# A linear-attention kernel with a folded feed-forward: one weight turned by VectorE in blocks, sign bits on GpSimd, seven products for one more chunk index, and a new order

## The chip, the cores and the metric

The kernel runs on one core of one Trainium2 chip. The metric is the device time of one execution in microseconds (us); below 2% a change of the median is called "within 2%".

## What is computed

Attention first: B=4 batches, H=8 heads, S=768 steps, D=48 numbers per head, with a state that decays by a constant w per head and row. Then a feed-forward on the 3072 rows of 384 numbers that come out of it.

```
for t in range(S):
    cur = einsum('bhd,bhe->bhde', u * kt, vt)
    y[:, :, t] = einsum('bhd,bhde->bhe', rt, state + cur)
    state = w * state + einsum('bhd,bhe->bhde', kt, vt)
x = y.transpose(0, 2, 1, 3).reshape(3072, 384)
a = x @ w1          # 384 x 1024
b = x @ w2          # 384 x 1024
out = ((a * b) @ w3) @ w_out     # 1024 x 1024, 1024 x 384
```

The four weights arrive as 64-bit floats; r, k, v, w, u as 32-bit floats.

## The kernel before, in words

**Units and chunks.** The steps are cut into six chunks of 128 steps; a chunk of one batch is a unit, so there are 24 units, four to a chunk index c. A unit's attention: k and r are scaled by tables of powers of w (`scale`, k in the order, L422 on VectorE), turned (by TensorE for units 0 to 4, T and R; by VectorE in 32x32 blocks with a trip through DRAM for the rest, x, y, z, l), multiplied (A, U, S, V), masked (m), and its rows are turned and put into `xT` (yt, yx). `odd_values` (vs, L678) copies v's odd heads to the other half of the partitions, on ScalarE.

**Opening.** Up to L306 a first section builds the tables: VectorE doubles powers in `both` (L292, L294), copies their first half to the second (L297, on ScalarE L298), TensorE turns four blocks for each of k and r (L303), and ScalarE puts both results into `pn_in` (L304).

**Weights.** There are 32 pieces: 8 strips of w1 and w2 (768 KB each), 8 row blocks of w_out (384 KB), 16 half row blocks of w3 (512 KB). A piece is fetched (W, L234) into one of three buffers and made a 32-bit float in five steps: magnitude (M, ScalarE L370), sign bits (N, VectorE L375), high part (H, VectorE L378), low part (L, ScalarE L382, the last to read the buffer), total (Q, VectorE L385). Since no function stands between w3 and w_out, the kernel folds them into one 1024 x 384 weight w34: for each of 8 row blocks j of w3, TensorE turns it (G, L398, eight 128x128 transposes in two halves), ScalarE takes the turned blocks out of PSUM (K, L403), TensorE multiplies by w_out (F, L408), ScalarE keeps the result (X, L411).

**Products.** For chunk indices 0 and 1, a and b are plain products (a, b, L740, up to 512 columns wide), with one ScalarE copy and one VectorE multiplication for each block of 128 rows. For chunk indices 2 to 5 they are made with seven products in place of eight over two thirds of the depth, from sums of weights (wa, wb) and of x (xs): `product_half` (pa, pb, L885 and L889, 256 columns wide) and `gather_half` (ga, gb, L900 to L916). The product with w34 uses seven products for all chunks (s, B, P, E, D). Z puts idle products on TensorE (L921).

**Order.** `ORDER` (L23) is a list of some 1,400 words; each names a step and its indices. The engines work in order, so the list fixes the order of the work of TensorE, ScalarE, VectorE and of SP, which issues the DMAs. When the opening has found w in a normal range, the listed program runs; else a plain one.

Of the kernel before, what the change touches and what calls it, by code (L numbers as in the profile page):

```python
# [8 lines left out]
F32 = mybir.dt.float32  # L9
BF16 = mybir.dt.bfloat16  # L10
I32 = mybir.dt.int32
U32 = mybir.dt.uint32
# [6 lines left out]
PE, ACT, DVE, SP = (getattr(mybir.EngineType, x) for x in ("PE", "Activation", "DVE", "SP"))  # L19
# [4 lines left out]
k.0 uw Z.1.0 R.0 vs.0 T.0 k.1 kr.2 U.0 t.0 v.2 r.0 i.0 T.1 j.0 ku.0 A.0 R.1 N.0 v.1 Au.0 t.1 r.1 S.0 m.0 kr.3 ku.1  # L24
mo.0 k.2 Z.4.0 A.1 M.0 Au.1 fe.0 R.2 W.1 m.1 vs.2 T.2 mo.1 U.2 W.2 t.2 H.0 V.0 r.2 Y.0 v.3 A.2 i.2 j.2 ku.2 U.1 yt.0
kr.4 i.1 j.1 S.2 L.0 Au.2 k.3 yx.0 vs.1 Z.1.0 R.3 m.2 T.3 M.1 mo.2 S.1 fe.2 fe.1 t.3 V.2 N.1 V.1 r.3 H.1 Y.2 A.3 W.3
Q.0 ku.3 yt.2 N.2 kr.5 vs.3 Z.2.0 Au.3 Y.1 m.3 yx.2 Z.2.0 U.3 mo.3 M.2 yt.1 v.5 i.3 k.4 S.3 yx.1 L.1 a.0.0.0 fe.3 H.2
Q.1 M.3 V.3 W.4 T.4 N.3 Y.3 R.4 H.3 kr.6 t.4 yt.3 b.0.1.0 r.4 j.3 ku.4 k.5 A.4 v.6 cz.1 L.3 Au.4 x.5 b.0.0.0 yx.3 L.2
Q.3 a.0.1.1 M.4 N.4 W.5 Q.2 vs.5 W.6 H.4 c.0.0.0 c.0.1.1 Z.3.0 b.0.2.2 m.4 v.4 L.4 mo.4 W.7 vs.6 Q.4 d.5 a.0.2.2
u.0.0.0 y.5 N.5 M.5 H.5 U.5 c.0.2.2 a.0.1.0 u.0.2.2 L.5 ub N.6 M.6 Q.5 b.0.1.1 vs.4 W.8 H.6 b.0.4.2 c.0.1.0 u.0.1.0  # L30
L.6 u.0.1.1 Q.6 W.9 M.7 N.7 a.0.4.2 H.7 z.5 e.5 L.7 f.5 Q.7 M.8 a.0.7.2 c.0.4.2 N.8 H.8 M.9 N.9 W.10 L.8 H.9 W.11 Q.8
L.9 b.0.6.2 Q.9 c.0.7.2 W.12 h.5 kr.7 l.5 d.6 e.6 f.6 a.0.0.1 M.10 N.10 H.10 b.0.7.2 N.11 M.11 kr.8 u.0.4.2 L.10 H.11
c.0.0.1 L.11 Q.10 N.12 M.12 Q.11 a.0.5.2 W.13 H.12 L.12 W.14 k.7 Q.12 W.15 b.0.0.1 d.7 c.0.5.2 e.7 kr.10 f.7 A.5
u.0.0.1 b.0.3.2 i.5 M.13 N.13 H.13 N.14 L.13 m.5 M.14 W.16 H.14 a.0.6.2 M.15 Q.13 L.14 N.15 W.17 H.15 Q.14 L.15 Q.15
W.18 c.0.6.2 j.5 b.0.5.2 u.0.6.2 M.16 N.16 H.16 u.0.7.2 M.17 a.0.3.2 N.17 L.16 H.17 W.19 Q.16 L.17 N.18 M.18 W.20 Q.17
G.0.0 c.0.3.2 H.18 G.0.1 K.0.0 U.4 u.0.3.2 L.18 k.6 K.0.1 W.21 F.0 N.19 M.19 kr.9 Q.18 H.19 N.20 M.20 i.4 L.19 H.20
W.22 Q.19 L.20 Q.20 M.21 W.23 N.21 G.1.0 X.0 H.21 G.1.1 K.1.0 U.6 j.4 K.1.1 G.2.0 x.6 L.21 F.1 K.2.0 W.24 Q.21 M.22
y.6 N.22 H.22 k.8 L.22 M.23 W.25 N.23 H.23 Q.22 L.23 N.24 W.26 G.2.1 Q.23 M.24 S.4 z.6 x.7 K.2.1 G.3.0 X.1 G.3.1 fe.4
H.24 K.3.0 F.2 M.25 N.25 u.0.5.2 L.24 H.25 K.3.1 Q.24 L.25 y.7 Q.25 M.26 W.28 N.26 H.26 W.27 d.8 l.6 e.8 kr.11 G.4.1
G.4.0 L.26 x.8 A.6 K.4.0 V.4 i.6 X.2 F.3 Y.4 cz.0 v.7 M.28 m.6 K.4.1 j.6 z.7 M.27 N.28 H.28 Q.26 L.28 Q.28 N.27 H.27  # L40
S.5 X.3 G.6.0 vs.7 fe.5 y.8 G.5.0 K.6.0 W.29 P.0.0.0 L.27 Q.27 W.30 V.5 W.31 l.7 yt.4 Y.5 G.5.1 g.6 yt.5 v.8 F.4 z.8
N.29 M.29 f.8 yx.4 H.29 yx.5 N.30 L.29 d.9 K.5.0 Q.29 K.5.1 N.31 g.7 S.6 e.9 G.6.1 fe.6 V.6 K.6.1 U.7 Y.6 v.9 M.30 A.7
k.9 F.6 M.31 X.4 m.7 kr.12 l.8 i.7 j.7 vs.8 x.9 vs.9 H.30 y.9 H.31 L.30 Q.30 L.31 U.8 X.6 Q.31 S.7 A.8 fe.7 k.10 V.7
yt.6 z.9 m.8 G.7.0 yx.6 i.8 G.7.1 K.7.0 F.5 j.8 K.7.1 g.8 x.10 v.10 s.0.1.0 y.10 s.0.1.1 Y.7 s.0.1.2 l.9 f.9 d.10 yt.7
X.5 e.10 kr.13 ps f.10 yx.7 g.9 s.0.1.3 z.10 d.11 b.1.0.2 e.11 vs.10 f.11 d.12 e.12 a.1.0.2 b.1.1.2 c.1.0.2 u.1.0.2
a.1.5.2 a.1.1.2 c.1.5.2 b.1.2.2 c.1.1.2 u.1.1.2 a.1.2.2 a.1.4.2 c.1.2.2 u.1.2.2 S.8 c.1.4.2 U.9 fe.8 l.10 A.9 k.11
b.1.4.2 i.9 kr.14 j.9 m.9 x.11 U.10 A.10 u.1.4.2 y.11 V.8 k.12 F.7 v.11 i.10 kr.15 j.10 m.10 Y.8 z.11 x.12 vs.11
a.1.3.2 B.0 X.7 E.0.0.0 s.0.0.0 y.12 B.1 a.1.6.2 s.0.0.1 c.1.3.2 B.3 B.2 s.0.0.2 P.0.0.2 c.1.6.2 wb.0 wb.1 P.0.1.4
s.0.0.3 wa.0 P.0.0.3 wa.1 wb.3 P.0.1.2 wa.3 E.0.0.2 U.11 E.0.0.3 P.0.0.4 k.13 x.13 P.0.1.0 E.0.0.4 y.13 b.1.6.2
E.0.1.0 E.0.1.2 b.1.5.2 u.1.6.2 P.0.1.1 u.1.5.2 s.1.0.0 P.0.0.5 s.1.0.1 s.1.0.3 a.1.7.2 s.1.0.2 E.0.1.1 E.0.0.6  # L50
E.0.0.5 D.0.0.0 P.0.0.1 wa.2 c.1.7.2 P.0.0.6 E.0.0.1 b.1.3.2 E.0.0.7 D.0.0.1 P.0.1.6 u.1.3.2 P.0.1.3 P.1.0.0 E.0.1.3
E.0.1.4 yt.8 E.1.0.0 P.0.1.5 g.10 b.1.7.2 E.0.1.6 E.0.1.7 f.12 yx.8 D.0.1.1 d.13 e.13 kr.16 P.1.1.0 u.1.7.2 s.1.1.0
P.1.0.4 s.1.1.1 E.1.1.0 s.1.1.3 P.1.0.2 s.1.1.2 wb.2 P.1.0.6 E.1.0.2 E.0.1.5 D.0.1.0 P.1.0.3 P.1.0.5 E.1.0.3 E.1.0.4
P.1.1.1 E.1.0.6 E.1.0.5 D.1.0.0 P.1.1.4 E.1.1.1 P.1.0.1 P.1.1.2 E.1.0.1 E.1.0.7 D.1.0.1 S.9 E.1.1.2 P.1.1.3 fe.9 l.11
z.12 V.9 E.1.1.3 Y.9 A.11 P.1.1.5 i.11 j.11 yt.9 m.11 v.12 P.1.1.6 yx.9 E.1.1.6 g.11 E.1.1.4 E.1.1.5 S.11 D.1.1.0
E.1.1.7 S.10 D.1.1.1 fe.11 V.11 fe.10 l.12 f.13 V.10 v.14 Y.11 U.12 v.13 vs.12 Y.10 yt.11 k.14 z.13 pa.2.0.0 yx.11
x.14 A.12 ga.2.0.0 yt.10 i.12 pa.2.0.1 yx.10 m.12 g.12 j.12 xs.2.0 S.12 y.14 xs.2.1 U.13 fe.12 xs.2.2 ga.2.0.5 V.12
xs.2.3 g.13 pa.2.0.5 d.14 v.15 e.14 kr.17 pa.2.1.4 Y.12 f.14 pa.2.0.4 ga.2.0.1 d.15 l.13 e.15 pa.2.0.6 ga.2.0.3 vs.13
A.13 z.14 f.15 yt.12 ga.2.0.2 i.13 pb.2.0.0 vs.15 m.13 yx.12 pa.2.0.7 j.13 g.14 k.15 pa.2.0.3 ga.2.0.4 kr.18 x.15
# [46 lines left out]
def kernel(  # L106
# [60 lines left out]

# [885 lines left out]
```

## Time and profile before

| what | value |
|---|---|
| runs | 507.63, 500.76, 507.02 us; median 507.02 |
| profiled execution | 501.81 us, its span 500.1 us |
| TensorE busy | 483.8 us |
| VectorE, ScalarE, GpSimd busy | 319.5, 202.7, 4.4 us |
| granted TensorE clock | 0.999 |

The profile is one execution, and its span runs from the first to the last instruction; 1.7 us of the execution's time lie around it. The three runs lie 6.9 us apart, and the profiled execution lies near the lowest. An fp32 product is two passes of TensorE, so 42 products of 512 columns show as 84 instructions; a transpose is one pass. Instructions of one engine overlap by a little, so that a group's busy time can be below count times mean.

### The profile page before, as it was taken

What the parts mean: (1) busy time and instruction counts of PE and PEld (TensorE: products, weight loads), DVE (VectorE), ACT (ScalarE), POOL (GpSimd) and SP (SyncE); (2) the same over time, 40 slices, a digit from 0 to 9 for tenths busy, and PEclk for the clock granted to TensorE, in tenths of its full rate; (3) what the DMA queues carried; (4) which work ended last, traced back from release to release, by engine and by line L of the source; (5) the groups of instructions that cost most, each with busy time, mean ns of one, the idle gap of its engine ahead of it and who ended that gap; (6) DMA issues with size and microseconds to landing.
All of it is one profiled execution on the core that took longest, in us unless ns stands there. A gap on an engine that the chain in (4) does not pass through costs nothing.

```text
span 500.1 us, 11978 instructions
## 1 busy us (share of the span) xinstructions
PE 483.8 (97%) x5066; PEld 384.4 (77%) x5066; DVE 319.5 (64%) x648; ACT 202.7 (41%) x470; POOL 4.4 (1%) x17
## 2 busy tenths in 40 slices
PE   6899999989999999999999999999999999999995
PEld 5786545657644586898888889989998889888895
DVE  5799999985951874539967894539462564524352
ACT  3887646768632100206852633062422232322300
POOL 3000000000000000000000000000000000000000
PEclk9999999999999999999999999999999999999999
DMA  8969787896620600216734435002300020000002
GB/s 193 241 167 287 209 224 227 250 262 172 159 64 1 174 33 20 59 49 177 167 108 108 113 99 139 32 33 70 90 33 31 1 81 17 27 25 0 2 1 69
DMA packets 97279, 52.72 MB, mean 105 GB/s; under 512 B 78144, under 2 KB 88640, under 8 KB 97216
## 3 DMA queue, kind: packets, MB, share of 16 engines
q1 hardware_dynamic: 96592, 51.85, 37.6%
q8 instruction: 42, 0.69, 0.6%
q14 instruction: 21, 0.17, 0.1%
q10 hardware_dynamic: 624, 0.00, 0.1%
HBM read 39.65 MB, written 12.19 MB: 104 GB/s over the span
## 4 chain that ended last, share of the span: by engine, by line
PE 86%; DMA 5%; DVE 4%; ACT 2%; issue 1%; SPq 0%; ACTq 0%; DVEq 0%
PE ps_accB L885 8%; PE ps_b L740 7%; PE ps_a L740 7%; PE ps_w L408 5%; PE ps_a11b L798 3%; PE ps_s1t L798 3%; PE ps_s4b L798 3%; PE ps_s3t L798 3%; PE ps_a22t L798 3%; PE ps_s2t L798 3%; PE ps_a12b L798 3%; PE ps_Ab L885 3%; PE ps_accB L889 3%; PE ps_a L551 3%; PE ps_accC L885 3%; PE ps_Aa L885 3%
## 5 line engine op out<-in xcount | busy, mean ns | idle before, releaser
L740 PE MATMUL ps_b<-xT,w 128*128 128x512 f32 (+1 forms) x108 | 44.4, 550 | 0.9 <-ACT a L746 0.7
L740 PE MATMUL ps_a<-xT,w 128*128 128x512 f32 (+1 forms) x108 | 43.7, 547 | 0.0
L408 PE MATMUL ps_w<-wo,w3T 128*128 128x384 f32 x128 | 43.0, 489 | 0.0
L885 PE MATMUL ps_accB<-x,w 128*128 128x256 f32 x128 | 36.5, 387 | 0.0
L740 PEld LDWEIGHTS ps_a<-xT,w 128*128 128x128 f32 x108 | 20.3, 190 | 20.5 <-issue 18.4
L408 PEld LDWEIGHTS ps_w<-wo,w3T 128*128 128x128 f32 x128 | 23.7, 190 | 15.1
L452 ACT ACTIVATE ynat<-vnat,dg 128x48 f32<-128x48 f32 x144 | 34.4, 325 | 0.8 <-PE ps_x L710 0.7
L740 PEld LDWEIGHTS ps_b<-xT,w 128*128 128x128 f32 x108 | 19.9, 190 | 18.7 <-issue 15.8
L508 ACT COPY kT<-tt 128x1024 f32<-128x1024 f32 x19 | 19.9, 1047 | 23.3 <-PE ps_y L671 21.0
L382 ACT ACTIVATE t<-raw 128x512 uint32<-128x512 uint32 (+2 forms) x32 | 22.6, 710 | 14.6 <-DVE wo L378 6.7
L885 PEld LDWEIGHTS ps_accB<-x,w 128*128 128x128 f32 x128 | 23.2, 190 | 5.0 <-ACT u2a L902 1.1
L422 DVE TENSOR_TENSOR krs<-krin,pn_in 128x768 f32<-128x768 f32 x24 | 22.9, 953 | 5.9 <-PE ps_a L544 3.3
L749 DVE TENSOR_TENSOR abt<-ps_b,a 128x512 f32<-128x512 f32 (+1 forms) x18 | 11.2, 628 | 20.5 <-ACT a L746 14.0
L746 ACT COPY a<-ps_a 128x512 f32<-128x512 f32 (+1 forms) x18 | 9.5, 535 | 33.4 <-PE ps_a L740 33.3
L716 ACT COPY xT<-ps_x 128x384 f32<-128x384 f32 x24 | 11.4, 478 | 28.8 <-PE ps_x L710 28.6
L678 ACT COPY vodd<-vnat 64x192 f32<-64x192 f32 x48 | 16.8, 350 | 13.8 <-DMA vnat<-in_v_dram 12.8
L551 PE MATMUL ps_a<-kT 64*64 64x64 f32 x768 | 16.8, 222 | 3.0 <-ACT kT L508 1.7
L813 ACT COPY m<-ps_a11b 128x192 f32<-128x192 f32 x12 | 3.8, 320 | 38.7 <-PE ps_a11b L798 38.7
L492 DVE STREAM_TRANSPOSE tr<-krs 128x768 f32<-128x768 f32 x19 | 18.4, 970 | 1.1 <-DMA scratch<-tr 0.9
L602 DVE COPY_PREDICATED AT<-later,ps_a 128x512 f32<-128x512 int32 x24 | 17.5, 730 | 2.5 <-PE ps_a L572 1.4
L889 PE MATMUL ps_accB<-xT,w 128*128 128x256 f32 x64 | 19.0, 379 | 0.0
L889 PE MATMUL ps_accC<-xT,w 128*128 128x256 f32 x64 | 19.0, 379 | 0.0
(191 smaller groups left out, 1069.0 us busy)
## 6 DMA issues: line engine op xcount, KB each, us to landing
raw<-in_moe_w_dram SPq DMA_DIRECT2D x16, 512.0 KB, 4.9
scratch<-tr SPq DMA_DIRECT2D x19, 384.0 KB, 3.1
raw<-in_moe_w_dram SPq DMA_DIRECT2D x8, 768.0 KB, 5.8
tt<-scratch SPq DMA_DIRECT2D x38, 128.0 KB, 3.1
krin<-in_k_dram SPq DMA_DIRECT2D x24, 192.0 KB, 3.8
krin<-in_r_dram SPq DMA_DIRECT2D x24, 192.0 KB, 4.3
vnat<-in_v_dram SPq DMA_DIRECT2D x24, 192.0 KB, 3.8
raw<-in_moe_w_out_dram SPq DMA_DIRECT2D x8, 384.0 KB, 3.6
```

Of the source, the lines that this page charges most:

```text
L382: nc.scalar.activation(out=part["t", i], in_=words(i)[0], func=COPY, scale=2.0 ** -29)
L408: nc.tensor.matmul(ps, lhsT=w3T[j][:, kc, :], rhs=wo[kc], start=(kc == 0), stop=(kc == KF - 1))
L422: nc.vector.tensor_mul(krs[n % NS][:, which, :, :D], kr[:, which], pn[:, which, :, :D])
L452: nc.scalar.activation(out=ynat[n][:, h, :], in_=vnat[n % NV][:, h, :], func=COPY, scale=dg[n][:, h:h + 1])
L492: nc.vector.transpose(out=blocks[n].rearrange("x m e t -> x e m t"), in_=krs[n % NS][:, :, :, :D])
L508: nc.scalar.copy(out=turned(n).rearrange("x g p (z t) -> x (g p) z t", t=Q), in_=tts.rearrange("x z e t -> x e z t"))
L551: nc.tensor.matmul(upper(n)[rows(a ^ i), i, p, :], lhsT=kT[n][rows(i), p, rows(a)], rhs=rT[n][rows(i), p, rows(a)], start=True, stop=True)
L602: nc.vector.copy_predicated(AT[n], later.bitcast(I32)[:, None, None, :].to_broadcast([C, 2, NP, T]), upper(n))
L740: nc.tensor.matmul(ps, lhsT=(w1 if x == "a" else w2)[:, z, q, js], rhs=xT[c][:, q, ts], start=(q == 0), stop=(q == KM - 1))
L798: nc.tensor.matmul(ps, lhsT=operand(c, j // 2, a)[:, j % 2, m * C:(m + 1) * C], rhs=w34[:, KH * (x == 1) + j, :DH] if x < 2 else made[b][: ...
L885: nc.tensor.matmul(ps, lhsT=quarter(w, g, i, x), rhs=(b11, b21, b22, t4, b12, t2, t3)[x], start=x in (0, 4) and i == 0, stop=True, skip_gr ...
L889: nc.tensor.matmul(ps, lhsT=wide_of[w][:, g + half * HZ, 2, i * P:(i + 1) * P], rhs=xT[c][:, 2, side * TH:(side + 1) * TH], start=False, s ...
```

## The change

- The 64 transposes of w3 on TensorE and the 16 ScalarE copies (K) go. `fold_turn` is now one VectorE transpose of 32x32 blocks for each half, SBUF to SBUF, 16 in all. So that blocks end in the right place, each fetch of a w3 piece becomes two DMAs of 256 KB that lay the four column blocks of 32 rows on the partitions, and w_out's rows are spread in the same way.
- Sign bits: N (VectorE, 32 times) goes; p is new: GpSimd multiplies the piece's high words, read as floats, by 0.0.
- vp is new: v's odd heads of units 0 to 5 are copied by GpSimd, not by ScalarE.
- Chunk index 1 uses pa, pb, ga, gb, xs: the eight pairs a.1, b.1 with c.1 and u.1 go. The sums of weights and of x, and two of the m1 tiles, now lie in the pool of the four w3 tiles, which stays open.
- Opening: the copies at L297 and L298 go, the eight transposes become 16 products of 64 columns each with the identity, and the second result is put by VectorE.
- Unit 0's scaling is split in two (ka, kb). Z: six words (13 idle products) become two (2 products).
- The list is new, and GpSimd is now also bound to it.

```diff
-k.0 uw Z.1.0 R.0 vs.0 T.0 k.1 kr.2 U.0 t.0 v.2 r.0 i.0 T.1 j.0 ku.0 A.0 R.1 N.0 v.1 Au.0 t.1 r.1 S.0 m.0 kr.3 ku.1
...
-k.9 F.6 M.31 X.4 m.7 kr.12 l.8 i.7 j.7 vs.8 x.9 vs.9 H.30 y.9 H.31 L.30 Q.30 L.31 U.8 X.6 Q.31 S.7 A.8 fe.7 k.10 V.7
-yt.6 z.9 m.8 G.7.0 yx.6 i.8 G.7.1 K.7.0 F.5 j.8 K.7.1 g.8 x.10 v.10 s.0.1.0 y.10 s.0.1.1 Y.7 s.0.1.2 l.9 f.9 d.10 yt.7
-X.5 e.10 kr.13 ps f.10 yx.7 g.9 s.0.1.3 z.10 d.11 b.1.0.2 e.11 vs.10 f.11 d.12 e.12 a.1.0.2 b.1.1.2 c.1.0.2 u.1.0.2
...
+v.1 kr.2 uw ka.0 k.1 vp.0 U.0 T.0 i.0 kb.0 T.1 t.0 v.2 j.0 p.0 ku.0 Z.1.1 R.0 kr.3 U.1 r.0 vp.1 i.1 t.1 j.1 Z.1.1 A.0
...
+p.14 d.8 e.8 H.14 L.14 p.16 M.16 Q.14 W.17 A.5 M.15 p.15 H.16 b.0.6.2 c.0.6.2 i.5 L.16 m.5 W.19 j.5 H.15 a.0.3.2 L.15
...
+p.30 V.6 m.7 M.31 F.6 i.7 j.7 v.9 H.30 Y.6 L.30 H.31 l.8 Q.30 G.7.0 L.31 s.0.1.0 vs.9 U.8 wa.0 A.8 X.6 wa.1 F.5 Q.31
+G.7.1 wa.3 wb.0 wa.2 s.0.1.1 i.8 k.9 yt.6 X.5 F.7 wb.1 yx.6 g.8 wb.3 x.9 k.10 y.9 s.0.1.2 j.8 m.8 S.7 s.0.0.0 X.7 U.9
+z.9 fe.7 B.0 V.7 P.0.1.0 Y.7 B.1 yt.7 v.10 E.0.1.0 s.0.0.1 pa.1.0.0 yx.7 xs.1.0 E.0.0.0 P.0.1.2 ga.1.0.0 xs.1.1 xs.1.2
...
-            queue.dma_start(out=landed[i], in_=pieces[i])
+            if i < NAB + KF:
+                queue.dma_start(out=landed[i] if i < NAB else landed[i][:, 0], in_=pieces[i])
+            else:
+                j, z = divmod(i - NAB - KF, NW3)
+                for f in range(2):
+                    queue.dma_start(out=landed[i][:, 0, f * DF // NBLOCK:(f + 1) * DF // NBLOCK],
+                                    in_=moe_w3[j * P:(j + 1) * P].rearrange("(f r) (q x) -> f q r x", r=Q, q=NBLOCK)[2 * z + f])
...
-        nc.vector.tensor_copy(out=both[:, 0, :, T:], in_=both[:, 0, :, :T])
-        nc.scalar.copy(out=both[:, 1, :, T:], in_=both[:, 1, :, :T])
...
-                nc.tensor.transpose(ps[:, p, :], both[:, g, p, :], ident)
-            nc.scalar.copy(out=pn_in[:, g].rearrange("t h d -> t (h d)"), in_=ps.rearrange("x p t -> x (p t)"))
+                for a in range(2):
+                    nc.tensor.matmul(ps[rows(a), p, :], lhsT=both[:, g, p, :T], rhs=ident, start=True, stop=True)
+            put = nc.vector.tensor_copy if g else nc.scalar.copy
+            put(out=pn_in[:, g].rearrange("t h d -> t (h d)"), in_=ps.rearrange("x p t -> x (p t)"))
...
+        def sign_by_scale(i, pool=False):
+            m, n = landed[i].shape[1:]
+            part["t", i] = once.tile([P, RAW], U32, tag="cv", bufs=2, name="t")[:, :m * n].rearrange("p (m n) -> p m n", m=m)
+            if pool:
+                nc.gpsimd.tensor_scalar(part["t", i].bitcast(F32), words(i)[1].bitcast(F32), 0.0, None, ALU.mult)
+            else:
+                nc.scalar.activation(out=part["t", i].bitcast(F32), in_=words(i)[1].bitcast(F32), func=COPY, scale=0.0)
...
         def fold_turn(j, h):
-            pst["w3", j, h] = ps = psT.tile([P, KF // 2, P], F32, tag="t", name=f"ps_w3T{j}_{h}")
-            for q in range(KF // 2):
-                kc = h * (KF // 2) + q
-                nc.tensor.transpose(ps[:, q, :], w3n[j][:, kc * P:(kc + 1) * P], ident)
-
-        def fold_put(j, h):
-            if h == 0:
-                w3T[j] = once.tile([P, KF, P], F32, tag="w3", bufs=4 if fast else 3, name=f"w3T{j}")
-            nc.scalar.copy(out=w3T[j][:, h * (KF // 2):(h + 1) * (KF // 2), :], in_=pst["w3", j, h])
+            if j not in w3T:
+                w3T[j] = wide_pool.tile([P, KF, P], F32, tag="w3", bufs=4 if fast else 3, name=f"w3T{j}")
+            by = w3n[j].rearrange("x (f c r) -> x f c r", f=NBLOCK, r=Q)[:, 2 * h:2 * h + 2]
+            nc.vector.transpose(out=w3T[j].rearrange("x c (f r) -> x f c r", r=Q)[:, 2 * h:2 * h + 2], in_=by)
...
-        def odd_values(n):
+        def odd_values(n, put=nc.scalar.copy):
...
-                made["w", w] = [room().tile([P, HZ, STRIP], F32, name=f"w{w}{i}") for i in (1, 2, 4)]
+                made["w", w] = [kept(3 * (w == "b") + i) for i in range(3)]
...
-            with tc.manual_schedule(engines={PE, ACT, DVE, SP}):
+            with tc.manual_schedule(engines={PE, ACT, DVE, SP, POOL}):
```

## The prediction

> **What bounds the kernel now.** I read the page's busy times, then the busy time by stage, then the chain of waits between 66 and 140 us, then the groups by shape. By stage (columns: length, then busy us and count of TensorE, its weight loads, VectorE, ScalarE, GpSimd; granted clock; DMA share; GB/s):
>
> ```profile
> 0.00:10.50 10.50, 6.63 (x41) 5.77 (x41) 5.33 (x34) 3.67 (x7) 4.37 (x17) 1.00 0.86 190
> 10.50:139.60 129.10, 123.73 (x1578) 82.20 (x1578) 110.78 (x205) 90.69 (x193) 0.00 (x0) 1.00 0.76 216
> 139.60:494.90 355.30, 353.43 (x3448) 296.39 (x3448) 203.00 (x411) 108.36 (x271) 0.00 (x0) 1.00 0.23 63
> 494.90:500.10 5.20, 0.00 (x0) 0.00 (x0) 0.34 (x1) 0.00 (x0) 0.00 (x0) 0.89 0.25 84
> ```
>
> 139.6 is where the last unit of chunk index 1 is in xT. After it the kernel is TensorE alone: 1.9 us idle in 355, VectorE 57% busy. Before it (10.5 to 139.6) TensorE idles only 5.4 us, but VectorE is busy 110.8 of 129.1 and the DMAs 76%. The chain of waits there leaves TensorE for a fetch and its conversion (start, duration, what):
>
> ```profile
> 73.37 5.06 DMA raw<-in_moe_w_dram
> 78.43 0.02 issue
> 78.45 0.70 ACT w3n L370
> 79.15 0.02 issue
> 79.17 0.70 DVE w3n L378
> 79.88 0.02 issue
> 79.90 0.70 ACT t L382
> 80.60 0.02 issue
> 80.61 4.98 DMA raw<-in_moe_w_dram
> ```
>
> So the first stage is a near tie of TensorE, VectorE and the weight loop (7.2 us a turn with three buffers), the second is TensorE's. The groups that the change touches (busy us, mean ns; then idle before):
>
> ```profile
> L398 PE MATMUL ps_w3T<-ident,w3n 128*128 128x128 f32 x64 | 9.2, 277 | 0.4 <-DVE w3n L385 0.4
> L403 ACT COPY w3T<-ps_w3T 128x512 f32<-128x512 f32 x16 | 9.0, 583 | 0.5 <-PE ps_w3T L398 0.4
> L375 DVE TENSOR_SCALAR t<-raw 128x512 uint32<-128x512 uint32 (+2 forms) x32 | 14.1, 439 | 1.3 <-DMA raw<-in_moe_w_dram 1.0
> L492 DVE STREAM_TRANSPOSE tr<-krs 128x768 f32<-128x768 f32 x19 | 18.4, 970 | 1.1 <-DMA scratch<-tr 0.9
> L678 ACT COPY vodd<-vnat 64x192 f32<-64x192 f32 x48 | 16.8, 350 | 13.8 <-DMA vnat<-in_v_dram 12.8
> ```
>
> And the only stretch where GpSimd and VectorE overlap, at the opening:
>
> ```profile
> 3.32 1.01 POOL L201 MEMSET AT<- 128x512 f32 x2
> 3.27 0.59 DVE L275 TENSOR_SCALAR wn_in<-wucol 128x4 f32<-128x4 f32 x1 [2.08 <-DMA wucol<-in_w_dram]
> 3.90 0.16 DVE L277 TENSOR_TENSOR wn_in<-wn_in 128x4 f32<-128x4 f32 x1
> ```
>
> The four-column TENSOR_SCALAR takes 0.59 us and ends when the first of the two memsets (mean 534 ns) ends; the next four-column operation, under the second memset, takes 0.16.
>
> [...]
>
> **The change part by part.**
>
> *w3's turning.* 64 transposes leave TensorE. Their busy sum is 9.2, but eight in a row take 0.87 us on the chain, 0.109 each: 7.0 us. ScalarE loses 9.0 us (hidden work). VectorE gains 16 transposes; by L492, 970 x 512/768 plus some fixed cost, 0.65 to 0.72: 11.2 us, in the stage where it is busiest. One PSUM round trip a half goes.
>
> *Chunk index 1.* Before: 16 products of three 512-column steps; the chain has 2.58 us for six passes, so 41.3 us. After: by (w, g), 22 products of 256 columns; two of them take 0.86 us (the chain's x4 lines), so 88 x 0.432 = 38.0. Gain 3.3 us of TensorE. VectorE pays 16 x 0.69 + 4 x 0.425 - 8 x 0.69 = 7.2 us more, ScalarE 18 x 0.585 - 8 x 0.58 = 5.9 more, both where they idle over 40%: nothing.
>
> *Sign bits.* VectorE loses 14.1 us; GpSimd gains 32 instructions, 17,408 columns in all. [...] High parts (H) wait for them in VectorE's in-order queue, and low part and next fetch stand behind H. Magnitude (0.68 to 0.92 on ScalarE) runs beside them and covers a sign of about that length; in the list there are mostly one or two VectorE operations more between p and H.
>
> *Ports.* H, Q, k, d, e have two SBUF inputs: 45.8 us for H and Q (22.9 each over three shapes) and some 16 for the rest, about half of VectorE's time up to 139.6. [...] I take 2.4 net[...].
>
> *Odd v, K.* ScalarE loses 4.2 us (12 x 0.35) beside K's 9.0 before 139.6: hidden, some slack for the magnitudes. GpSimd gains 12 short copies (0.35 to 0.5 each) ahead of signs in its queue.
>
> *Opening.* VectorE's copy L297 (0.30) goes from the chain; eight transposes (0.64 for four on the chain) become 16 two-pass products. By four idle passes in 0.45 us a pass is 0.11: 3.6 us if one after another, half if the two 64-column halves run together. The second put moves to VectorE (0.6) ahead of ka (0.55 in place of 0.95 for k.0). Between 0 and 1.5 us late; I take 0, since list and loads go on beside it. Z's 11 fewer idle products (2.5 us) filled waits: nothing.
>
> *Fetches.* 16 more DMA issues of about 0.4 us on SP, and 2 KB rows in place of 4 KB. The 2 KB rows of w1, w2 land 768 KB in 5.8 us, w3's 512 KB took 4.9: no loss in bytes, and the loads queued behind on SP get up to 6.4 us in all over 60 us of slack-rich queue. Nothing.
>
> *The sum.* Both lists, priced with these rows up to yx.7 (139.6): VectorE -14.1 (N) - 5.2 (k.0, now ka and kb; x of unit 10 and d, e, f of 9 and 10, now later) + 11.2 (turning) + 9.2 (weight sums, s, B, earlier, and ka, kb) = +1.1 us. TensorE -7.5 - 2.5 (Z) + 7.9 (F.7, U.9, P.0.1.0, pa.1.0.0, now earlier) = -2.1. What TensorE has after yx.7 falls by these 7.9 and 3.3: 11.2. So the span is 500.1 - 11.2 + the shift of yx.7. VectorE sets that shift: +1.1 + 2.4 = +3.5. Span 492.4, with the 1.7 us around it 494.1. The profiled 501.81 lies near the lowest of runs that reach 507.63 (median 507.02), so a median may lie up to 5 above the sum; I write 495.
>
> **Rivals.**
>
> *TensorE's shift instead (0.10).* VectorE's freed idle time absorbs the ports and yx.7 moves by -2.1: span 486.8, 488.5 us. For: ScalarE has 13 us less to do before it. Against: VectorE's sum rises, and its queue was already 86% full.
>
> *The port takes it back (0.27).* [...] yx.7 at +11 to +14, span 500 to 503, time 501 to 508. For: the 0.59 us line. [...]
>
> *Signs become the bound (0.13), slower.* One sign per piece, in order: if it takes longer than its cover (magnitude 0.68 plus one or two VectorE operations, about 1.1 us), the excess is paid in VectorE's queue for each of 32 pieces. To be over 2% slower (517) it must cost some 22 us above my sum: 0.7 us a piece, thus about 1.8 us for 512 columns. The copy taken per column gives 1.85: the edge of the bound, not its middle.
>
> *The seven products don't gain:* excluded; 256 columns cost half of 512 in the chain.
>
> **How the numbers follow.** My case has 0.50, its own range 489 to 500. Below it the 0.10 at 487 to 489, above it 0.27 and 0.13. 2%, about what a measurement of this kernel can tell from no change, lies at 496.9. Faster: 0.40 of my case and the 0.10, 0.50. Same: 0.10 of mine and 0.25 of the port's, 0.35. Slower: 0.13 and 0.02. The range 487 to 508 leaves out the slow rival and little else.
>
> **What would show it.** Right: no L398 group; 16 transposes of 0.65 to 0.72 us; TensorE busy about 470; yx.7 between 140 and 146; two-input operations of VectorE with longer means than now (H above 0.687) by a little. Wrong: signs of over 1.2 us with H waiting on GpSimd; TensorE idle over 10 us between 80 and 145; or idle after 145, where I assume 2.

## The result, and the profile after

The changed kernel takes 560.52 us (median of four runs, 556.4 to 565.09), the kernel before beside it 505.21. The ratio is 1.1079, 95% interval 1.0954 to 1.1204: slower, by far outside the range of 487 to 508. Ratios here and below compare fast runs alone (within 1.5% of the fastest run of the same kernel), so they are not the quotients of the medians. The profiled execution took 559.54 us, its span is 557.8 us.

First the stages, as in the prediction, cut at the end of yx.7, now at 209.2 us (same columns: length, then busy us and count of TensorE, weight loads, VectorE, ScalarE, GpSimd; granted clock; DMA share; GB/s):

```profile
0.00:10.50 10.50, 7.97 (x62) 7.34 (x62) 5.06 (x33) 2.07 (x3) 5.08 (x19) 1.00 0.83 182
10.50:209.20 198.70, 143.48 (x1554) 88.75 (x1554) 116.20 (x196) 79.74 (x168) 59.77 (x42) 0.84 0.47 137
209.20:552.60 343.40, 341.98 (x3470) 306.60 (x3468) 206.88 (x417) 114.37 (x281) 0.00 (x0) 1.00 0.25 68
552.60:557.80 5.20, 0.30 (x2) 0.00 (x1) 0.36 (x1) 0.00 (x0) 0.00 (x0) 0.82 0.15 48
```

After yx.7 the kernel needs 557.8 - 209.2 = 348.6 us; before it was 360.5. The forecast gain of 11.2 us is there, 11.9. The first stage is 69.6 us longer (209.2 against 139.6), and it is full of holes: TensorE idles 55 us of 198.7, VectorE 82, and the DMAs carry 137 GB/s where they carried 216. The same 45 us of both kernels, where the fetches of w_out and w3 run, before:

```profile
70.00:115.00 45.00, 42.16 (x342) 25.72 (x343) 39.18 (x75) 29.59 (x54) 0.00 (x0) 1.00 0.78 234
```

and after:

```profile
70.00:115.00 45.00, 29.97 (x89) 13.42 (x87) 17.80 (x34) 11.47 (x22) 12.18 (x9) 0.76 0.29 101
```

101 GB/s at a DMA share of 0.29. The DMA view of after between 60 and 150 us shows a ceiling. Its first row is the busy share of the 16 DMA engines in tenths, slice by slice:

```profile
DMA  2222252343222222222222222222222222225253
GB/s 104 104 102 104 98 139 81 122 120 66 81 93 102 104 103 101 102 96 102 101 102 102 101 102 86 83 108 102 102 102 102 102 101 101 96 101 164 100 153 71
```

A row of twos, with 102 GB/s beside it: about a quarter of the 16 engines' time, slice after slice. The chain of waits shows what that does (start, duration, what):

```profile
105.27 11.79 DMA raw<-in_moe_w_dram
...
117.22 1.54 POOL t L391
...
118.79 0.70 DVE w3n L396
...
119.51 0.67 ACT t L400
...
120.20 0.53 SPq L243
...
120.78 12.28 DMA raw<-in_moe_w_dram
```

It is the loop that the prediction read at 73 to 81 us: landing, conversion, next fetch. It took 7.2 us a turn and takes 15.5. Three pieces, one for each buffer, are 1.57 MB, and 1.57 MB at 0.102 MB per us is 15.4 us: the transfer alone accounts for the turn. The groups of the change, from the page (busy us, mean ns; then idle before and what ended it):

```profile
L391 POOL TENSOR_SCALAR t<-raw 128x512 f32<-128x512 f32 (+2 forms) x32 | 54.5, 1705 | 121.1 <-DMA raw<-in_moe_w_dram 75.2
L396 DVE SCALAR_TENSOR_TENSOR w3n<-w3n,t 128x512 uint32<-128x512 uint32 x16 | 10.9, 691 | 44.4 <-POOL t L391 44.4
```

and from the list of groups with the shapes kept apart:

```profile
L417 DVE STREAM_TRANSPOSE w3T<-w3n 128x512 f32<-128x512 f32 x16 | 11.1, 703 | 0.2
L391 POOL TENSOR_SCALAR t<-raw 128x512 f32<-128x512 f32 x16 | 25.1, 1568 | 72.2 <-DMA raw<-in_moe_w_dram 60.8 <-DVE w3n L403 5.9 <-DVE AT L697 5.5
```

Here is a trap. By these lines VectorE's high part waits 44.4 us for GpSimd, and a sign of 512 columns takes 1.57 us, near the 1.85 that the prediction names as the edge of its bound. The rival of the signs seems proven. But GpSimd itself waits 75.2 us for the DMAs: the wait is handed on. Two theories were therefore tried against each other: placement (the new fetches are slow) and signs (GpSimd is slow).

### The profile page after: what moved, and what is told of

Its sections match the earlier page's. It is cut to its first block, busy times and chain, and to the rows that moved or that the text cites. A ratio compares the mean times of both kernels' runs of the same rounds, so it can differ in the third digit from the quotient of the medians.

```text
span 557.8 us, 12087 instructions
## 1 busy us (share of the span) xinstructions
PE 493.7 (89%) x5084; PEld 402.7 (72%) x5084; DVE 328.5 (59%) x645; ACT 196.2 (35%) x450; POOL 64.9 (12%) x61
## 4 chain that ended last, share of the span: by engine, by line
PE 66%; DMA 20%; DVE 4%; SPq 3%; ACT 3%; POOL 2%; issue 1%; ACTq 0%; POOLq 0%; DVEq 0%
DMA raw<-in_moe_w_dram 10%; PE ps_accB L917 9%; DMA raw<-in_moe_w_out_dram 5%; DMA tt<-scratch 5%; PE ps_Ab L917 3%; PE ps_accC L917 3%; PE ps_accC L921 3%; PE ps_accB L921 3%; PE ps_s4b L812 3%; PE ps_s3t L812 3%; PE ps_s1t L812 3%; PE ps_s2t L812 3%; PE ps_a22t L812 3%; PE ps_Aa L917 3%; PE ps_a12b L812 3%; PE ps_a11b L812 3%
## 5 line engine op out<-in xcount | busy, mean ns | idle before, releaser
L391 POOL TENSOR_SCALAR t<-raw 128x512 f32<-128x512 f32 (+2 forms) x32 | 54.5, 1705 | 121.1 <-DMA raw<-in_moe_w_dram 75.2
L917 PE MATMUL ps_accB<-sumw,w 128*128 128x256 f32 x160 | 45.6, 387 | 0.0
L754 PE MATMUL ps_a<-xT,w 128*128 128x512 f32 (+1 forms) x60 | 29.8, 651 | 11.9 <-DVE abt L763 11.9
L396 DVE SCALAR_TENSOR_TENSOR w3n<-w3n,t 128x512 uint32<-128x512 uint32 x16 | 10.9, 691 | 44.4 <-POOL t L391 44.4
L917 PEld LDWEIGHTS ps_accB<-sumw,w 128*128 128x128 f32 x160 | 28.9, 190 | 5.5 <-ACT u3a L934 1.1
L754 PE MATMUL ps_b<-xT,w 128*128 128x512 f32 (+1 forms) x60 | 25.1, 567 | 7.9 <-ACT a L760 7.0
L436 DVE TENSOR_TENSOR krs<-krin,pn_in 128x768 f32<-128x768 f32 (+1 forms) x25 | 23.3, 937 | 9.5 <-PE ps_a L565 5.3
L685 PE MATMUL ps_y<-st,kT 64*64 64x48 f32 x320 | 14.5, 226 | 13.0 <-ACT w L425 11.9
L685 PEld LDWEIGHTS ps_y<-st,kT 64*64 64x64 f32 x320 | 11.8, 138 | 18.4 <-ACT w L425 12.2
L917 PE MATMUL ps_accC<-xT,sumw 128*128 128x256 f32 x80 | 24.1, 383 | 0.1
L917 PE MATMUL ps_Ab<-xT,w 128*128 128x256 f32 x80 | 22.7, 385 | 0.3 <-DVE ynat L717 0.3
```

What stands on the lines that cost most here:

```text
L391: nc.gpsimd.tensor_scalar(part["t", i].bitcast(F32), words(i)[1].bitcast(F32), 0.0, None, ALU.mult)
L436: nc.vector.tensor_mul(krs[n % NS][:, which, :, :D], kr[:, which], pn[:, which, :, :D])
L685: nc.tensor.matmul(yt[n][i][rows(a), p, :], lhsT=rw[rows(i), p, rows(a)], rhs=(half[n % 2] if a else st[b][(c + 1) % 2])[rows(i), p, :], s ...
L754: nc.tensor.matmul(ps, lhsT=(w1 if x == "a" else w2)[:, z, q, js], rhs=xT[c][:, q, ts], start=(q == 0), stop=(q == KM - 1))
L917: nc.tensor.matmul(ps, lhsT=quarter(w, g, i, x), rhs=(b11, b21, b22, t4, b12, t2, t3)[x], start=x in (0, 4) and i == 0, stop=True, skip_gr ...
```

## The experiments

All were timed beside the kernel before on the same chip, in groups on different chips, so that across groups the ratios are the safer measure; "rest" is the span less the end of yx.7, from each kernel's own profile.

| kernel | median us | ratio (95%) | yx.7 ends | rest |
|---|---|---|---|---|
| after | 560.52 | 1.1079 (1.0954 to 1.1204) | 209.2 | 348.6 |
| e1, fetches over 32 partitions | 507.59 | 1.0043 (1.0018 to 1.0068) | 157.0 | 349.2 |
| e2, signs on VectorE | 563.15 | 1.1164 (1.1118 to 1.1209) | 212.6 | 348.6 |
| e3, both | 506.75 | 1.0035 (1.0000 to 1.0069) | 157.1 | 348.9 |
| e4, before with the new fetches | 576.35 | 1.1400 (1.1359 to 1.1441) | 215.5 | 361.3 |
| e5, before with GpSimd's signs | 507.97 | 1.0064 (1.0043 to 1.0085) | 144.6 | 360.3 |
| e6, after with the old fetches | 507.73 | 1.0047 (1.0020 to 1.0075) | 156.7 | 349.3 |
| e7, and signs on VectorE | 504.87 | 1.0009 (0.9975 to 1.0042) | 153.2 | 349.7 |
| e8, and odd v on ScalarE | 505.06 | 0.9988 (0.9954 to 1.0023) | 151.7 | 348.9 |
| e9, e3 with the old first part | 515.42 | 1.0219 (1.0169 to 1.0270) | 153.5 | 359.8 |
| e10, e3 with the old opening | 504.72 | 0.9994 (0.9970 to 1.0018) | 154.1 | 349.0 |
| e11, old list, w3 by VectorE | 516.42 | 1.0224 (1.0175 to 1.0273) | 155.0 | 360.9 |
| e12, before, w3 by VectorE | 512.51 | 1.0159 (1.0126 to 1.0192) | 149.1 | 359.3 |
| e13, before, w3 not turned | 505.32 | 1.0023 (0.9997 to 1.0048) | 142.4 | 359.6 |
| e14, e12 with GpSimd's signs | 512.25 | 1.0146 (1.0088 to 1.0205) | 150.0 | 359.5 |
| e15, before without signs | 502.72 | 0.9978 (0.9953 to 1.0004) | 139.8 | 361.1 |
| e16, e12 without signs | 505.89 | 1.0028 (1.0006 to 1.0050) | 144.8 | 358.7 |
| e17, sevens alone | 501.01 | 0.9941 (0.9917 to 0.9964) | 144.4 | 357.0 |
| e18, e13 with half of w3 fetched | 503.16 | 0.9979 (0.9956 to 1.0003) | 143.1 | 360.1 |

### Fetches or signs

**e1.** The same placement, but each piece of w_out and w3 by four DMAs, one for each group of 32 partitions, so that no access has the four blocks as its outermost dimension.

```diff
-for f in range(2):
-    queue.dma_start(out=landed[i][:, 0, f * DF // NBLOCK:(f + 1) * DF // NBLOCK],
-                    in_=moe_w3[...].rearrange("(f r) (q x) -> f q r x", ...)[2 * z + f])
+for q in range(NBLOCK):
+    queue.dma_start(out=landed[i][q * Q:(q + 1) * Q, 0].rearrange("r (f x) -> r f x", f=2),
+                    in_=moe_w3[...].rearrange("(f r) (q x) -> q r f x", ...)[q][:, 2 * z:2 * z + 2])
```

> The changed kernel, but each piece of w_out and w3 is fetched by four DMAs of 32 partitions (slowest dimension 32) in place of DMAs whose slowest dimension is the 4 column blocks; the bytes end in the same places. Placement theory (the four-deep outer dimension keeps a fetch on about 4 of the 16 DMA engines, about 100 GB/s, and the weight loop waits for it): the DMA rate between 50 and 150 us returns to over 200 GB/s, a weight fetch lands in about 5 us, time 495 to 515 us. Sign theory (GpSimd's 1.57 us per sign sets the loop): the rate rises but the time stays above 540 us.

507.59 us. 53 us are back, inside the time range of the placement theory, from the shape of the DMAs alone, and yx.7 moves from 209.2 to 157.0. The same 45 us now:

```profile
70.00:115.00 45.00, 40.82 (x242) 21.52 (x244) 35.74 (x62) 21.83 (x38) 24.78 (x16) 0.96 0.73 194
```

**e2.** After with the words p as N, VectorE's sign bits:

> The changed kernel with sign bits back on VectorE, at the same places of the list; fetches as in the changed kernel. Placement theory: each turn of the weight loop (some 15.5 us for three pieces) loses the 1.1 us by which a sign on GpSimd is longer than on VectorE, about 8 turns, so 8 to 12 us: 545 to 553 us, DMA rate still about 100 GB/s. Sign theory: 495 to 515 us.

563.15 us, not faster than after. Both expectations missed: even the few us of the placement theory didn't come. In this loop, where the transfer alone accounts for 15.4 of the 15.5 us of a turn, signs of 0.44 us on VectorE in place of 1.71 on GpSimd (means over all shapes, before and after) gained nothing.

**e3.** Both edits:

> Both edits: fetches by four DMAs of 32 partitions, sign bits on VectorE. Placement theory: what is left is the removed TensorE work, span 486 to 495, time 488 to 500 us. Sign theory: the same value; a third cause (the list, the kept pools, the opening) would show as a time above 505 us.

506.75 us; between e1 and e3 lies 0.8 us, within the intervals. The signs did not make the 55 us. But it is not 488 to 500 either: as the expectation has it, a time above 505 means a third cause.

**e4.** The kernel before, with only the new fetches (its blocks then lie in other places than its products expect, so what it computes is changed):

> The kernel before with only the new fetches: w_out and w3 pieces laid on the partitions by DMAs whose slowest dimension is 4. Rows and columns then no longer match the transposes on TensorE, so its output isn't the reference's; the work and its order are those of before. Placement theory: 540 to 560 us, about 100 GB/s between 50 and 140 us. Sign theory: 500 to 508 us.

576.35 us, 71 above the kernel before, more than either expected. Its yx.7 is 6 us later than after's, and it lacks the shorter rest (361.3 against 348.6). Its chain of waits has no GpSimd in it:

```profile
80.43 14.70 DMA raw<-in_moe_w_out_dram
...
95.15 0.55 ACT wo L378
95.70 0.44 ACT t L390
...
99.17 13.28 DMA raw<-in_moe_w_dram
```

So the fetches are enough for the loss, and without them it is gone. What differs stands in the traces' packets. Of w3's packets in before (4 KB each, 70 to 115 us), 16 are on the way at once more often than any other number, none aside; in after (2 KB each, 80 to 150 us) it is four, for 64% of the time, and never more than seven. Between 124 and 130 us of after, with only w3's fetches on the way, the DMA share is 0.26 (4.2 of 16 engines) at 102 GB/s. Over the 45 us from 70 on, with everything else counted in, it is 0.29 and 101 GB/s in after and 0.34 and 108 in e4, in place of 0.78 and 234 in before. Four blocks outermost went with four packets at a time; why they do, the runs don't show. The prediction did not reckon with it.

### With the fetches repaired: where did 11 us go?

**e5.** The kernel before with signs on GpSimd only:

> The kernel before with only the sign bits moved to GpSimd, at N's places of its list; its fetches use all DMA engines. Sign theory in its weak form (1.57 us for 512 columns where magnitude covers 0.7): in the stretches where a conversion ends the chain of waits, up to 1.1 us a turn of three pieces, 3 to 12 us slower, 508 to 517 us. If the queue hides a sign as it seemed to in e1_spread against e3_both: 504 to 508 us.

507.97 us, some 3 us for GpSimd's slower signs and what they hold up, at the edge between the two ranges. Without the slow DMAs GpSimd's line shows what the signs cost:

```profile
L375 POOL TENSOR_SCALAR t<-raw 128x512 f32<-128x512 f32 x16 | 26.2, 1639 | 24.7 <-DMA raw<-in_moe_w_dram 9.4 <-DVE w3n L385 8.9 <-ACT t L382 4.7
L378 DVE SCALAR_TENSOR_TENSOR w3n<-w3n,t 128x512 uint32<-128x512 uint32 x16 | 11.9, 748 | 6.4 <-POOL t L375 4.5 <-ACT w3n L370 1.4 <-ACT w3T L403 0.4
```

The high part waits 4.5 us for GpSimd, not 44, and takes 748 ns in place of 687. If GpSimd's work beside it is the reason, that is 16 x 0.061 = 1 us here. How uneven it can be, the profile of after shows: of its eight high parts of 768 columns the one at 50.2 us, with GpSimd at a sign all the while, takes 1.56 us; the others take 0.91 to 0.96 us, two of them with GpSimd at a sign for 0.79 and 0.92 us of it.

**e6, e7, e8.** After with the old fetches, one DMA for each piece, so that w_out's and w3's rows don't stand where the turned blocks need them (the work is the same, the values are not); then also p as N; then also vp as vs:

> The changed kernel with the fetches of before: one DMA for a piece, 128 rows outermost. Rows of w_out and blocks of w3 then don't match, so its output isn't the reference's; all other work and the list are those of the changed kernel. If what e1_spread has left (chunk index 1's input complete at 156 us in place of 139.6) is the 1.3 us that three more DMA issues add to each fetch: 490 to 498 us. If it is the list's first part (loads, opening, odd v): 502 to 508 us.

> e6 with sign bits on VectorE; output not the reference's for the same reason. If signs on GpSimd are hidden: within 3 us of e6_plain_fetch. If the weight loop sees them once fetches are quick: 5 to 12 us below it.

> e7 with v's odd heads of units 0 to 5 back on ScalarE; output not the reference's for the same reason. If waits of GpSimd's copies for v hold units 1 to 4 up (TensorE stood 3.2 us before one of these in e3_both): 2 to 5 us below e7_plain_sign_vector. If it is v's load that is late, whoever copies: the same.

507.73, 504.87 and 505.06 us. e6 is equal to e1: SP's 72 issues more do not hold 10 us, and one DMA for a piece does as well as four, so that the number of DMAs was not what the 53 us came from. Signs on VectorE bring 2 to 3 us (by the ratios and by the medians), inside the 3 us set for "hidden"; odd v nothing outside the intervals. e8 is the changed kernel without the slow DMAs and without what the change gave to GpSimd, and it is level with the kernel before. Its rest is 348.9, 11.6 below before; its yx.7 is 12.1 later. The loss lies in the first stage and is as large as the gain of the second.

**e9, e10, e11.** e3 with before's list as far as yx.7; e3 with before's opening; and before's list throughout, with w3 turned by VectorE:

> The changed kernel with fetches over 32 partitions and all sign bits on VectorE (the third experiment), and with the list of before as far as the word yx.7 (without its K words, F.4 ahead of G.5.0), then the new list's words that are left. Theory A, the new list's order of the first stage gives the gain back: yx.7 at 131 to 136 us in place of 156, and 494 to 500 us in all. Theory B, VectorE's turning of w3 gives it back: yx.7 at 139 or later and 501 to 505 us. Theory C, the new opening gives it back: 502 to 506 us, with yx.7 over 142.

> The third experiment (fetches over 32 partitions, all sign bits on VectorE) with the opening of before: two copies of the tables and eight transposes for sixteen products. Theory A (order of the list): 505 to 508 us, as the third experiment's 506.75. Theory C (the opening): 499 to 503 us. Theory B says nothing of it.

> The list of before throughout (without its K words, F.4 ahead of G.5.0), so without the seven products for chunk index 1; of the change only w3's turning by VectorE, with fetches over 32 partitions, and the new opening. Theory A: TensorE is the bound and loses 7.0 us, 497 to 501 us. Theory B: VectorE's 11.2 us more push the first stage back, 503 to 508 us. Theory C: 502 to 506 us with the loss ahead of 15 us.

515.42, 504.72 and 516.42 us. e9 and e11 lie above every range, e10 between two. Theory A fell: with the old first part yx.7 comes 3.6 us earlier than in e3, not 20 or more, and since the work that the new list moves ahead then stands behind it, the rest is 10.9 us longer and the whole 9 us worse. The opening costs some 2 us (e10 against e3, intervals that overlap). And the turning, meant to save 7 us, came with 11 us more than the kernel before. The fetches in four DMAs, the new opening and new places of some buffers are in that too, so the next runs took them out. (e9's rest holds the work of e17's below: TensorE is busy 350.1 us in it, there 349.9. It is 2.8 us longer in its one profile; why stays open.)

### What sets the length of the first stage

**e12, e13, e14.** All on the kernel before with its own fetches and opening.

```diff
 e12: fold_turn
-nc.tensor.transpose(ps[:, q, :], w3n[j][...], ident)      # and the K words
+nc.vector.transpose(out=w3T[j]..., in_=w3n[j]...)
 e13: fold_put, fold_turn left empty
-nc.scalar.copy(out=w3T[j][...], in_=pst["w3", j, h])
+nc.scalar.copy(out=w3T[j][...], in_=w3n[j]...)
```

> The kernel before, its fetches (one DMA for each piece), its opening and its list, with w3 turned by VectorE as the only part of the change (no K words, F.4 ahead of G.5.0). The fetches don't place the blocks, so w3's rows stand in the wrong order and the output is not the reference's; the instructions are those of the turning. Theory B (VectorE, 90% busy from 50 to 100 us, pays what TensorE saves): 503 to 510 us. Theory D (the eleven us more of the run with the turning alone came from the fetches in four DMAs): 496 to 501 us.

> The kernel before without TensorE's turning of w3: the K words copy w3 as it stands (ScalarE, from SBUF), so 7.0 us of TensorE and the waits on it go, nothing is added to VectorE, and the output is not the reference's. Theory E, TensorE sets the pace of the first stage: 497 to 500 us. Theory F, it waits there for the chain that makes w3 (fetch, ScalarE and VectorE) and the turning only filled that wait: 503 to 506 us, and the saved time stands as TensorE's waits on w3n or w3T.

> The run with w3 turned by VectorE in the kernel before, and the sign bits of all pieces on GpSimd; the output is not the reference's for the same reason. Theory B (VectorE is the limit): below the run without GpSimd by 3 to 8 us, 497 to 503 us. Otherwise: equal to it or up to 4 us above it, as GpSimd's part in the chain of one piece is 0.9 us longer.

e13: 505.32 us, ratio 1.0023. 7.0 us of TensorE work are gone, nothing is added, and nothing is gained. The waits of TensorE between 70 and 150 us (us in total, times, longest) show where they went:

```profile
PE ps_w L405 <- ACT w L408: 1.8, 1, 1.8
PE ps_w L405 <- ACT w3T L400: 1.6, 1, 1.6
PE ps_y L691 <- DVE AT L680: 1.0, 2, 0.8
PE ps_a11b L795 <- ACT w L408: 1.0, 1, 1.0
PE ps_x L707 <- DVE ynat L700: 0.7, 1, 0.7
PE ps_b L737 <- ACT a L743: 0.7, 1, 0.7
PE ps_u L541 <- ACT a L743: 0.6, 1, 0.6
PE ps_w L405 <- ACT xT L713: 0.6, 1, 0.6
PE ps_w L405 <- ACT t L382: 0.5, 1, 0.5
```

8.5 us in small waits for ScalarE and VectorE, where the kernel before has 3.0: 5.5 of the 7.0 us stand there as waiting. Between 75 and 125 us TensorE is busy 47.44 us before and 42.11 in e13. Theory E fell: TensorE was nearly full there, but taking work from it did not shorten the stage. The time is that of theory F, but not its waits: of the 8.5 us only 1.6 name w3n or w3T.

e12: 512.51 us, ratio 1.0159, that is 7.2 us above e13. It differs from e13 in 11 us of VectorE transposes in place of ScalarE's copies, and in the list by the words K and the place of F.4. So most of what is added to VectorE in this stage is paid; it is a little over theory B's range, and theory D fell. e14: 512.25, GpSimd's signs relieve VectorE by 14.1 us and bring nothing, as its second range has it.

**e15, e16, e18.** The signs left out (the high part reads the magnitude twice), on the kernel before and on e12; and e13 with half of each w3 piece fetched:

> The kernel before without the sign bits: the 32 VectorE instructions N go and nothing takes their place (the high part combines the magnitude with itself, so the output is not the reference's). VectorE loses 14.1 us of its first stage. Theory G, VectorE sets the pace of the first stage: 14.1 us times the 0.64 that the turning's 11.2 us cost (7.2 us against the run without turning), 494 to 498 us. Theory H, the fetch loop of three buffers sets it (landing, magnitude, high part, low part, next fetch; the sign lies beside the magnitude): 502 to 506 us.

> The same on the kernel before with w3 turned by VectorE (512.5 us with signs on VectorE, 512.25 with signs on GpSimd): the signs cost nothing anywhere, the output is not the reference's. Theory G: the change's plan works once the signs are free, 497 to 504 us, and GpSimd's slow signs had eaten the relief. Theory H: 509 to 513 us, and relieving VectorE could not have paid for the turning.

> The kernel before without TensorE's turning of w3 (505.3 us), and with only the first 256 of the 512 columns of each w3 piece fetched, the converting steps unchanged; the output is not the reference's. It halves 8.4 MB of transfers, so that a piece lands in some 2.5 to 3 us in place of 5. Theory H (the fetch loop holds the first stage, so that the 7.0 us of TensorE were only wait): 496 to 501 us, the 7 us show at last. Theory G (VectorE's queue and the order of the list hold it): 503 to 506 us, no change.

e15: 502.72 us, ratio 0.9978. 14.1 us less of VectorE are worth 1 to 2 us (by the ratio and by the medians; the interval reaches 2.4): theory G in its simple form fell, H's range holds. e16: 505.89, 6.6 us below e12, between the ranges of G and H. On a VectorE loaded with the turning, free signs do bring a relief, and e14 shows that GpSimd's signs at 1.6 us for 512 columns eat just that (512.25 against 505.89, 6.4 us). e18: 503.16, ratio 0.9979. The bytes of w3 halved and 7.0 us of TensorE gone bring 1 to 2 us, some 2 us of them against e13: theory H fell as well, and G's range holds here. The fetches did become faster (256 KB in 3.4 us by the page's issue rows, before 512 KB in 4.9):

```profile
70.00:115.00 45.00, 40.57 (x328) 22.62 (x326) 39.79 (x78) 28.87 (x53) 0.00 (x0) 1.00 0.59 174
```

but VectorE is still busy 39.79 of 45 us, 88%.

So TensorE's turning, VectorE's signs, and the turning with half of w3's transfers can each be taken away with a gain of some 2 us or less. We read this as a tie of TensorE, VectorE and the fetch loop, tied together by a list in which each engine waits in order for the others. Which chain remains when all are relieved was not tried and stays open; nor was a list made anew for any of these kernels.

**What fills the stage.** The granted clock has a part in it. In e7 TensorE stands still for 2.5 us from 63.2 us on and for 3.6 us from 111.5 us on, and from 66.2 and 114 us on it is granted half of its clock for 3.4 and 6.8 us (after the length comes TensorE's busy time; the clock is the third from the end):

```profile
62.80:66.20 3.40, 0.94 (x3) 0.49 (x3) 3.40 (x8) 2.01 (x5) 0.00 (x0) 1.00 0.60 205
66.20:69.60 3.40, 3.40 (x7) 2.01 (x6) 3.25 (x8) 1.59 (x4) 0.00 (x0) 0.50 0.63 194
110.60:114.00 3.40, 0.93 (x61) 0.80 (x51) 0.76 (x3) 0.00 (x0) 0.00 (x0) 1.00 0.91 245
114.00:120.80 6.80, 5.68 (x70) 3.95 (x71) 6.11 (x12) 5.74 (x13) 0.00 (x0) 0.50 0.83 249
```

The profile of after has such stretches too, with the products slower in them: those of 384 columns for w34 that start between 164.5 and 166.6 us, at a granted clock of 0.50, have a median of 847 ns (four records), the thirteen from 166.6 to 170.6 us, at 1.00, one of 486. The time up to yx.7 can thus be split for each profile into TensorE's idle time, half of its busy time in such stretches (an estimate of what the clock cost) and all else:

| kernel | yx.7 ends | idle | clock | all else |
|---|---|---|---|---|
| before | 139.6 | 9.2 | 0.0 | 130.4 |
| e7 | 153.2 | 16.7 | 7.7 | 128.8 |
| e8 | 151.7 | 17.1 | 3.3 | 131.3 |
| e13 | 142.4 | 15.9 | 1.6 | 124.9 |
| e12 | 149.1 | 18.8 | 5.9 | 124.4 |
| e16 | 144.8 | 14.8 | 5.3 | 124.7 |
| e18 | 143.1 | 14.2 | 4.4 | 124.5 |

In e13 the 5.5 us by which the last column is shorter came back as 6.7 us of waits and 1.6 of clock. Single profiles scatter, but the executions without a profile point the same way: the mean clock of an execution was 0.994 for the kernel before and 0.983 and 0.984 for e7 and e8 beside it, some 5 us of 503 withheld (an upper estimate of the cost); e12 had 0.983 where e13 had 0.991, 4 us of the 7.2 that VectorE's turning cost. No run holds the clock fixed, so how much the waits alone would have cost is not shown.

### The part that pays

**e17.** The kernel before to the end of yx.7, then the new list's words, with seven products for chunk index 1:

> Of the change only the seven products for chunk index 1: the fetches, the opening, w3's turning by TensorE and the list up to yx.7 are those of before, the rest is the new list's words that are left; the complete computation. TensorE alone sets the second stage, so its 3.3 us come off whole: 500 to 503 us, ratio 0.991 to 0.996. If the moved-ahead work of the new list (7.9 us) was needed to keep TensorE fed there: 504 to 507 us.

501.01 us, ratio 0.9941 (0.9917 to 0.9964), the lowest of all. The stages, cut at 144.4:

```profile
0.00:10.50 10.50, 7.17 (x41) 6.31 (x41) 5.34 (x34) 3.66 (x7) 4.36 (x17) 1.00 0.86 188
10.50:144.40 133.90, 125.88 (x1579) 84.48 (x1580) 110.58 (x205) 90.58 (x192) 0.00 (x0) 0.99 0.73 209
144.40:496.20 351.80, 349.92 (x3527) 311.67 (x3526) 210.79 (x421) 113.97 (x281) 0.00 (x0) 1.00 0.24 64
```

The rest is 357.0 us, 3.5 below before, and TensorE idles 1.9 us in it. This profiled execution has a later yx.7 than that of before, 144.4 against 139.6, with the same work in front of it. The medians do not show these 5 us: the profile of before was taken of an execution 2.8 us below its median (501.81 against 504.6), that of e17 of one 2.1 us above (503.12 against 501.01). Single profiles of this stage scatter by that much.

## Why the prediction was wrong, point by point

**Fetches: the step that failed.** "No loss in bytes ... Nothing" compared row lengths (2 KB rows of w1 and w2 against the new 2 KB rows), and row length was not what decided. w1 and w2's DMAs have 128 partitions outermost, the new ones four blocks. The cost is 53 us (after against e1), from the loop's turn of 15.5 us in place of 7.2. No line of the trace of before told what four blocks would do; that "Nothing" was the author's estimate. A quarter of what the trace of before gives would be 234 / 0.78 / 4 = 75 GB/s as an estimate, and 102 was measured.

**The sum after yx.7: right.** 11.2 us less forecast, 11.9 measured, 11.3 to 11.6 in e1 and e8.

**The shift of yx.7: wrong also without the fetches.** The step "TensorE ... = -2.1. VectorE sets that shift: +1.1 + 2.4 = +3.5" gives 143.1; e1 has 157.0, e8 151.7. It set -7.5 for the turning (7.0 in its own working) against +7.9 for work moved ahead of yx.7, as if TensorE's time could be exchanged there. e13 shows that the saving is worth nothing in the kernel before; if so here too, the 7.9 stay as a loss. And it set VectorE's lighter load (-14.1) against its new one (+11.2): e15 shows that the first is worth 1 to 2 us, e12 against e13 that the second costs 7.2. 139.6 + 7.9 + 7.2 = 154.7 is then what these terms give for signs on VectorE, and e7 has 153.2. With single profiles that scatter by 5 us this is no proof that the terms add. What e7's profile does show is that the 13.6 us are 7.5 of idle and 7.7 of clock, less 1.6 of work; the prediction had no term for either, and its durations are those at a clock of 1.00. The sum took engine totals in a stage where no total was the bound; "a near tie", the prediction's own words, should have meant that a saving there counts as nothing and an addition in part.

**Sign bits: longer than their cover, mostly hidden.** 1.57 us for 512 columns, 54.5 us in all, against a cover of about 1.1 us a piece. The trace of before had no such operation of GpSimd: a memset of 512 columns took 534 ns there, and a 64-column copy 232 ns, taken per column 1.86 us for 512. The size that the prediction gave a sign was the author's estimate. Two of the prediction's own signs of being wrong appeared, signs of over 1.2 us with H waiting for GpSimd and TensorE idle over 10 us between 80 and 145, yet the cause they pointed to was not the one. The rival "Signs become the bound" put the decision at 1.8 us; at 1.57 to 1.68 it costs 1 to 3 us against VectorE's signs (e1 against e3, e5, e6 against e7) and 6.4 against signs that are free (e14 against e16), far from the 22 that this rival needed.

**"Ports": the size not contradicted, the cause not shown.** The 2.4 us net, for VectorE's operations with two SBUF inputs and GpSimd's signs holding each other up, were the author's estimate; all that the trace of before had for it was the 0.59 us line, an operation with one input. The high part takes 708 ns in e1 beside GpSimd against 670 in e3, 748 in e5 against 687 in before; the whole effect of the signs on GpSimd, this in it, is some 3 us, and no run parts the two.

**w3's turning, Chunk index 1, Odd v, Opening.** 703 ns for a turning (0.65 to 0.72 forecast). 3.3 us forecast for the sevens, 3.0 by e17's ratio, 3.6 by the medians of e17 and its kernel before (504.6), 3.5 by the rest. Odd v hidden: e7 and e8 agree within their intervals. Opening: taken at 0, by e10 some 2 us late; the 16 products take 1.97 us in the profile of after, near half of the 3.6.

**TensorE's busy time** was to be about 470 and is 493.7. The granted clock is 0.84 in the first stage of after where it was 1.00; with half of TensorE's busy time at half clock taken off (19.3 us, worked out as in the table above) 474 remain, so the count of work was near and the clock was left out. In the 45 us from 70 on the granted clock was 0.76 in after, with TensorE busy 29.97 us, 0.96 in e1 with 40.82 and 1.00 in before with 42.16.

## What to carry to other kernels

Before a DMA's access is rearranged, look at its outermost dimension, not only at the length of its rows (rows of 2 KB both times here, 128 partitions or four blocks outermost), and check the first profile for a DMA share that sits at a fixed fraction (0.26 here). In a stage where several engines are nearly full and wait for each other in a fixed order, do not count work taken from one of them as time gained (7.0 us of TensorE gave nothing here), and count work added to one as paid in good part (7.2 of 11 us); look first for a saving in the stage that a single engine sets. Look at the granted clock beside the busy time: in e7 holes of 2.5 and 3.6 us in TensorE went with 3.4 and 6.8 us at half of it. When a new wait names an engine, ask what that engine waits for before blaming it.

## What the runs showed of the hardware that was not expected

- Between 70 and 115 us, with the fetches of w_out and w3 in DMAs with four blocks outermost, 101 GB/s were moved (after; 108 in e4), with 128 partitions outermost 234 (before), and with four DMAs of 32 partitions for each piece 194 (e1).
- GpSimd's fp32 multiplication by a constant took 1.57 us for 512 columns with inputs 8 bytes apart (2.46 us for 768, 1.23 for 384 columns), 3.1 to 3.2 ns a column (after), and a copy of 64x192 took 0.50 us (after) and 0.39 us (e1), on ScalarE 0.35 (before).
- Beside it VectorE's high part of 512 columns, with two SBUF inputs, was on average only 38 and 61 ns (6 and 9%) longer (e1 against e3, e5 against before); in after a single one of 768 columns took 1.56 us against 0.91 to 0.96 for the other seven.
- In e7 two stretches of 3.4 us in which TensorE was busy 0.94 and 0.93 us were followed by 3.4 and 6.8 us at a granted clock of 0.50; in after two of 3.4 us with 0.82 and 0.68 us busy, from 61.0 and 74.6 us on, by 6.8 us each at 0.50.
